# Reordering an SSM-plus-local-attention kernel: part A's corrections and outputs interleaved anew, the sine table and some loads moved, negated maxima spread by ScalarE

## The chip, the cores and the metric

The kernel runs on one core of a Trainium2 chip. The metric is the device time of one execution in microseconds (us); lower is better. An execution also has a mean granted TensorE clock, written here as a share of full speed (1.0, 0.989, ...). Times are compared at the same clock wherever that is possible, and the text says where it is not.

Engines: PE is TensorE (PEld its weight loads), DVE is VectorE, ACT is ScalarE, POOL is GpSimd, SP is SyncE, which here only issues DMAs.

## The reference

Two independent layers read their own input of 2048 positions by 448 channels; their results are concatenated.

```python
def _A_ref(x, Lambda_re, ..., Dskip):              # state space layer, P = 448 complex states
    Lam_bar = exp(exp(log_dt) * Lam)
    Bu = einsum("bld,pd->blp", x, B_bar)
    for t in range(L):                             # 2048 steps
        h = Lam_bar * h + Bu[:, t, :];  hs.append(h)
    return 2.0 * einsum("blp,dp->bld", stack(hs), Cmat).real + x * Dskip

def _B_ref(x, wqkv, wo):                           # dilated sliding attention
    q, k, v = split(x @ wqkv)                      # 16 heads of 28
    # each position sees 8 positions: itself and 2, 4, ... 14 before it
    attn = softmax(where(mask, q . k[pos - 2w] * scale, -1e9))
    return (sum over w of attn[w] * v[pos - 2w]) @ wo
```

## The kernel before

The instructions of PE, DVE, ACT and SP are issued in program order, written by hand in one function, `plan`. Each engine works through its queue in that order, so an instruction that has to wait blocks all that stand behind it on the same engine (in experiment 9 one correction waits 1.02 us at the head of PE's queue, and the matmuls behind it come late: DVE then stands 1.30 us for them). `run(gen, n)` emits the next n pieces of a generator: `fill` are query and key projections, `vp` value projections, `tb` the sine and cosine tables of part A, `sb` part A's input matrix, `pv` the products of attention and values on DVE.

Part A treats the 2048 positions as 128 chunks of 16. A position in a chunk is 4a + b. `local(b, m)` computes states within four positions for one of seven state blocks m (PE, evicted by ACT). `last`, `rot`, `scan`, `back` carry the state between chunks (PE and DVE alternately). `groups` then adds the carried state to the states b = 3 (PE, then DVE), `correct(b, ...)` to those of b = 0, 1, 2, and `y(a, b)` makes the output of one position.

```python
def max_r(self, c):                    # part B: the negated maximum over the 8 window places
    V.tensor_reduce(mx[:], ..., op=ALU.max, axis=mybir.AxisListType.X, negate=True)
    V.tensor_copy(self.mxb[:], mx[:].unsqueeze(2).to_broadcast([NCH, 4, W, H]))   # spread to 8

def correct(self, b, add, ms):
    for m in ms:
        st = add == "V"
        if not st:                                             # "A": PE adds the old state itself,
            nc.tensor.matmul(ps, lhsT=cx.ident[:], rhs=h_, start=True, stop=False)
        ...                                                    # matmul with the carried states
        if st: nc.vector.tensor_tensor(h_, ps, h_, op=ALU.add) # "V": DVE adds
        else:  nc.scalar.copy(h_, ps)                          # "A": ACT only copies

# ---- plan(), cuts marked ----
    for g, which in first:                 # first four projections of part B
        b.proj_m(0, g, which, [3])
        b.proj_e(0, g, which, "A")         # evicted by ACT
    p0 = proj(0, (2, 3))
    run(tb)                                # sine table load and three sines on ACT
    run(p0, 3)
    ...
    run(sb, 7)
    for j in range(0, T, 3):               # softmax normalisation: PE transposes, DVE divides
        b.norm(j)
        run(vp, 2)
    run(vp, 16)
    a.load_c()
    b.load_wo()
    a.setup_c()                            # DMA transposes of C
    pv = chain(b.pv(0, 4), b.pv(4, 8), b.pv(8, 12), b.pv(12, 14), b.pv(14, 16))
    for ms in ((0, 1), (2, 3)):
        loc(*((b_, m) for b_ in (0, 2, 1, 3) for m in ms))
    run(pv, 20)                            # each pv() ends with the DMA transposes into oT
    ...
    a.rot(r_[1], 0)
    a.scan(r_[1])
    a.groups(range(2, 4))
    b.out(2)
    run(pv, 1)
    a.correct(1, "A", range(0, 4))
    a.back(rb[1])
    a.correct(0, "A", range(0, 4))
    run(pv, 1)
    a.groups(range(4, 7))
    a.correct(1, "A", range(4, 7))
    a.correct(0, "A", range(4, 7))
    for a_ in range(4):
        a.y(a_, 3)
    run(pv, 8)
    a.correct(2, "V", range(7))
    ...
    for a_ in range(4):
        a.y(a_, 2)
    b.out(12)
    run(pv, 99)
    b.out(14, "AV")
```

Of the kernel before, what the change touches and what calls it, by code (L numbers as in the profile page):

```python
# [17 lines left out]
D = 448  # L18
# [74 lines left out]
class PartB:  # L93
# [5 lines left out]

    def load_x(self, c):  # L100
        if c == 0:
            self.xT = self.pool.tile([NCH, KT, S], bf16, name="xbT", tag="xT")
        sl = slice(c * CH, (c + 1) * CH)
        x_ = self.B_x[0][sl, :]
        self.nc.sync.dma_start_transpose(out=self.xT[:, 0:3, sl], in_=x_[:, 0:3 * NCH])
        self.nc.sync.dma_start_transpose(out=self.xT[:, 3, sl], in_=x_[:, D - NCH:D])

# [165 lines left out]
    def max_r(self, c):  # L273
        V, pool = self.nc.vector, self.pool
        mx = pool.tile([NCH, 4, H], bf16, name="mx", tag="mx", bufs=2)
        self.mxb = pool.tile([NCH, 4, W, H], bf16, name="mxb", tag="mxb", bufs=2)
        V.tensor_reduce(mx[:], self.pt[:].rearrange("p n (w h) -> p n h w", h=H), op=ALU.max,
                        axis=mybir.AxisListType.X, negate=True)
        V.tensor_copy(self.mxb[:], mx[:].unsqueeze(2).to_broadcast([NCH, 4, W, H]))

# [72 lines left out]

    def out(self, j, engs="AA"):
        nc, i, oT = self.nc, j % 4, self.oT[j - j % 4]
        yb = self.pool.tile([NCH, 2, D], bf16, name="yb", tag="yb", bufs=2)
        for n in range(2):
            ps = self.cx.ps([NCH, D], f32, "wo_ps", "lg")
            for k in range(KT):
                nc.tensor.matmul(ps[:], lhsT=oT[:, NSL * (i // 2) + 3 * n + k, :], rhs=self.wo_p[:, KT * n + k, :],  # L360
                                 start=(k == 0), stop=(k == KT - 1))
            self.cx.ev(engs[n], yb[:, n, :], ps[:])
        nc.sync.dma_start(self.out_b[:, j:j + 2, :], yb[:])


class PartA:
# [94 lines left out]
    def tables(self):  # L461
# [10 lines left out]
        self.rho = sm("rho")  # L472
        nc.scalar.activation(self.rho[:], at2[:, 0, :], ACT.Exp, scale=float(T))
        turn = sm("turn")
        V.tensor_scalar(turn[:], at2[:, 1, :], T / TWO_PI, None, op0=ALU.mult)
# [9 lines left out]
        nc.scalar.activation(shE[:], fr[:], ACT.Sin, scale=math.pi)  # L485
        nc.scalar.activation(sn[:], fr[:, :, NCH:], ACT.Sin, scale=-TWO_PI)
        nc.scalar.activation(self.sinE[:], fr[:, :, 0:NCH], ACT.Sin, scale=self.sgn[:])
        yield
# [14 lines left out]
    def params_g(self):  # L503
        nc, G, ident = self.nc, self.nc.vector, self.cx.ident
        lre, lim, rden, Scat, dsk = self.lre, self.lim, self.rden, self.Scat, self.dsk
        la_re, la_im = self.pw_re[:, 0, :], self.pw_im[:, 0, :]
# [13 lines left out]
        G.tensor_tensor(g_im[:], g_im[:], rden[:], op=ALU.mult)  # L520
        self.mat("g", self.rot_rows("Sg", g_re, g_im)[:], G)
        self.Dg = self.pool.tile([NCH, KT, NCH], bf16, name="Dg")
        for k in range(KT):
            nc.scalar.activation(self.Dg[:, k, :], ident[:], ACT.Copy, scale=dsk[:, k:k + 1])

# [24 lines left out]
    def setup_b(self, engs):  # L550
        nc, cx, pool = self.nc, self.cx, self.pool
        self.Bcat = pool.tile([NCH, KT, NM, NCH], bf16, name="Bcat")
        for i in range(NM):
            pt = cx.ps([NCH, KT, NCH], f32, "pt_b", "pt")
            for k in range(KT):
                nc.tensor.matmul(pt[:, k, :], lhsT=self.bX[:, i, KOFF[k]:KOFF[k] + NCH], rhs=self.mats["g"][:, i, :],
                                 start=(k == 0), stop=(k == KT - 1), skip_group_check=True)
            cx.ev(engs[i % len(engs)], self.Bcat[:, :, i, :], pt[:])
            if i == NM - 1:
                nc.gpsimd.memset(self.Bcat[0:PL, 3], 0.0)  # L560
            yield
# [127 lines left out]
def body(ctx: ExitStack, tc: tile.TileContext, A_x, A_Lre, A_Lim, A_Bre, A_Bim, A_Cre, A_Cim, A_logdt, A_Dskip,  # L689
# [7 lines left out]
    a = PartA(cx, A_x, A_Lre, A_Lim, A_Bre, A_Bim, A_Cre, A_Cim, A_logdt, A_Dskip, out_v[:, :, 0:D])  # L697
    b.load_w(1, nc.sync)
    a.load_params()
    b.load_w(0, nc.scalar)  # L700
    b.load_x(0)
    b.load_wt()
# [15 lines left out]
def run(gen, n=1):  # L718
    for _ in range(n):
        next(gen, None)  # L720


def plan(a, b, cx, pool):
# [25 lines left out]
    run(tb)  # L749
    first = [(g, which) for g in (0, 1) for which in (1, 0)]  # L750
    for g, which in first:
        b.proj_m(0, g, which, range(3))
    for g, which in first:
        b.proj_m(0, g, which, [3])
        b.proj_e(0, g, which, "A")
    p0 = proj(0, (2, 3))
    run(tb)
    run(p0, 3)
    pr = [None, None]
    for g in range(NG):  # L760
        for s in range(2):
            pr[s] = b.prod(0, s, g, g + 1)
            if g == 2 and s == 0:
                b.prod_t(0)
    run(fill, 7)
    b.sums(0, 0, pr[0])
    run(fill, 1)
    b.sums(0, 1, pr[1])
    run(tb, 2)
    run(xl, 4)  # L770
    b.vd = pool.tile([NCH, TJ, DH, H], bf16, name="vd", tag="vd")
    b.zero_halo(b.vd)
    p = b.prod(1, 0)
    b.prod_t(1)
    run(fill, 2)
    b.max_t(0)
    b.max_r(0)
    run(fill, 4)
    b.sums(1, 0, p)
    b.max_s(0)  # L780
    p = b.prod(1, 1)
    a.skip()
    a.params_g()
    run(fill, 3)
    b.sums(1, 1, p)
    p = b.prod(2, 0)
    b.prod_t(2)
    run(fill, 1)
    b.max_t(1)
    b.max_r(1)  # L790
    run(fill, 3)
    b.sums(2, 0, p)
    b.max_s(1)
    p = b.prod(2, 1)
    a.params_m([0], nc.vector)
    run(vp, 3)
    b.sums(2, 1, p)
# [7 lines left out]
    run(sb, 1)  # L805
    b.sums(3, 0, p)
    b.max_s(2)
    p = b.prod(3, 1)
    run(sb, 2)
    run(vp, 2)  # L810
    b.sums(3, 1, p)
    run(vp, 1)
    run(sb, 1)
    b.max_t(3)
    a.alloc()
    a.params_m([1, 2], nc.vector)
    b.max_r(3)
    a.params_m([3, 4], nc.vector)
    run(vp, 1)
    b.max_s(3)  # L820
    run(vp, 1)
    run(sb, 7)

    def loc(*bm):
        for b_, m in bm:
            a.local(b_, m)

    for j in range(0, T, 3):
        b.norm(j)
        run(vp, 2)  # L830
    run(vp, 16)
    a.load_c()
    b.load_wo()
    a.setup_c()
    pv = chain(b.pv(0, 4), b.pv(4, 8), b.pv(8, 12), b.pv(12, 14), b.pv(14, 16))
    for ms in ((0, 1), (2, 3)):
        loc(*((b_, m) for b_ in (0, 2, 1, 3) for m in ms))
    run(pv, 20)
    a.scan_alloc()
# [10 lines left out]
    a.back(rb[0])  # L850
    run(pv, 4)
    a.last(r[1])
    run(pv, 1)
    a.groups(range(0, 2))
    b.out(0)
    a.rot(r_[1], 0)
    a.scan(r_[1])
    a.groups(range(2, 4))
    b.out(2)
    run(pv, 1)  # L860
    a.correct(1, "A", range(0, 4))
    a.back(rb[1])
    a.correct(0, "A", range(0, 4))
    run(pv, 1)
    a.groups(range(4, 7))
    a.correct(1, "A", range(4, 7))
    a.correct(0, "A", range(4, 7))
    for a_ in range(4):
        a.y(a_, 3)
    run(pv, 8)  # L870
    a.correct(2, "V", range(7))
    for a_ in range(4):
        a.y(a_, 1)
    run(pv, 8)
    b.out(4)
    b.out(6)
    for a_ in range(4):
        a.y(a_, 0)
    run(pv, 15)
    b.out(8)  # L880
    b.out(10)
    for a_ in range(4):
        a.y(a_, 2)
    b.out(12)
    run(pv, 99)
    b.out(14, "AV")

# [30 lines left out]
```

## Time and profile before

| | before |
|---|---|
| time, median of three executions | 153.34 us (153.12 to 153.38) |
| PE busy | 137.3 us, 90% |
| DVE busy | 132.5 us, 87% |
| first product of attention and values on DVE | 65.93 us |
| last matmul ends | 147.96 us |

The first view is the page's line of busy times: engine, us, share of the span, instructions.

```profile
PE 137.3 (90%) x910; PEld 71.4 (47%) x917; DVE 132.5 (87%) x185; ACT 85.1 (56%) x167; POOL 19.4 (13%) x59
```

Two engines are nearly full, so the averages do not say which one limits. The table of windows does. Its columns are the window and its length, then the busy us (and instructions) of PE, PEld, DVE, ACT and POOL, the granted clock, the DMA share and GB/s.

```profile
20.00:40.00 20.00, 19.11 (x156) 8.43 (x158) 19.53 (x32) 15.88 (x35) 3.39 (x8) 1.00 0.32 63
40.00:66.00 26.00, 23.14 (x217) 15.49 (x217) 23.89 (x28) 16.75 (x34) 0.97 (x2) 1.00 0.32 75
66.00:92.00 26.00, 25.90 (x129) 12.12 (x130) 25.97 (x30) 14.53 (x25) 0.00 (x0) 1.00 0.54 114
```

From 20 to 66 us DVE is busy for 43.4 of 46 us and PE for 42.3. From 66 to 92 us both are full. What can be gained lies therefore in the gaps and in work that can be taken off both. The timeline shows the gaps. Its columns are start, duration (us), engine, source line, operation, output and inputs, shapes, count; the bracket is the idle time of that engine just before, and what ended it.

```profile
12.69 1.28 ACT L485 ACT_TABLE_LOAD   x1
13.98 0.98 ACT L485 ACTIVATE shE<-fr 128x931 f32<-128x931 f32 x1
16.54 1.89 PE L192 MATMUL qk_ps<-xbT,wqkv_nat 128*128 128x512 bf16 x8 [1.68 <-ACT kT L83]
17.27 1.25 DVE L238 TENSOR_TENSOR pr<-qT,kT 128x2048 bf16<-128x2048 bf16 x1 [0.71 <-ACT qT L83]
...
60.86 0.46 DVE L303 RECIPROCAL rec<-tp 128x48 f32<-128x48 f32 x1 [0.64 <-PE tp L300]
62.57 0.46 DVE L303 RECIPROCAL rec<-tp 128x48 f32<-128x48 f32 x1 [0.66 <-PE tp L300]
65.93 1.08 DVE L320 TENSOR_TENSOR pvb<-attn,vd 128x1792 bf16<-128x1792 bf16 x1
...
98.20 1.69 PE L360 MATMUL wo_ps<-wo_p,oT 128*128 128x448 bf16 x8 [1.02 <-DMA oT<-pvb]
...
146.27 1.69 PE L360 MATMUL wo_ps<-wo_p,oT 128*128 128x448 bf16 x8 [0.72 <-ACT oT L351]
148.00 0.62 DVE L88 CAST yb<-wo_ps 128x448 bf16<-128x448 f32 x1 [1.39 <-PE wo_ps L360]
```

ScalarE loads a table and makes sines in the midst of the first evictions, and PE (1.68 us) and DVE (0.71 us) wait for those evictions. DVE waits twice for PE in the normalisation, because two value projections stand between two steps. PE waits 1.02 us for a DMA transpose. The last output projection waits 0.72 us for the eviction of its transposed input.

### The profile page before, as it was taken

How to read it: one execution, taken by the hardware profiler on the slowest of the kernel's cores; microseconds unless marked ns; L12 is line 12 of the kernel's file. 1: busy time of each engine (PE TensorE's matmuls, PEld its weight loads, DVE VectorE, ACT ScalarE, POOL GpSimd, SP SyncE). 2: the span in 40 equal slices, each digit the busy share in tenths (PEclk: the TensorE clock that was granted, in tenths of full speed). 3: DMA queues.
4: the chain of work that ended last, by engine and by line, in shares of the span. 5: the costliest groups of instructions: out<-in, count | busy, mean ns of one | idle time of the engine just before them, and what ended most of it. 6: DMA issues, size and time to landing. Idle time of an engine off the chain costs nothing.

```text
span 151.8 us, 2532 instructions
## 1 busy us (share of the span) xinstructions
PE 137.3 (90%) x910; PEld 71.4 (47%) x917; DVE 132.5 (87%) x185; ACT 85.1 (56%) x167; POOL 19.4 (13%) x59
## 2 busy tenths in 40 slices
PE   6899599997999789899999999699999899999980
PEld 5243244442466557644445444354554455555530
DVE  0298799999999988799999999998899999999701
ACT  3129996799678558544564544249852126254350
POOL 8189992000000001000000000000000000000000
PEclk9999999999999999999999999999999999999999
DMA  4999991222222142529762358612511013929321
GB/s 114 252 213 196 190 193 35 36 62 44 43 60 44 39 135 55 146 43 226 109 114 67 70 130 110 121 60 73 109 35 60 30 60 102 233 91 151 128 91 60
DMA packets 42282, 15.67 MB, mean 103 GB/s; under 512 B 34770, under 2 KB 41824, under 8 KB 42269
## 3 DMA queue, kind: packets, MB, share of 16 engines
q1 hardware_dynamic: 41806, 15.16, 45.5%
q10 hardware_dynamic: 463, 0.35, 1.2%
q8 instruction: 7, 0.11, 0.3%
q14 instruction: 6, 0.05, 0.1%
HBM read 3.62 MB, written 3.67 MB: 48 GB/s over the span
## 4 chain that ended last, share of the span: by engine, by line
PE 70%; DVE 11%; ACT 11%; DMA 4%; issue 2%; SPq 0%; DVEq 0%
PE u_ps L584 16%; PE y_ps L681 14%; PE qk_ps L192 10%; PE v_ps L218 6%; PE wo_ps L360 6%; DMA xbT<-in_B_x_dram 4%; ACT kT L83 3%; PE lg L254 3%; PE y_ps L678 2%; ACT qT L83 2%; DVE pr L238 2%; PE u_ps L587 2%; PE co L656 2%; PE co L660 2%; DVE u L662 2%
## 5 line engine op out<-in xcount | busy, mean ns | idle before, releaser
L332 DVE TENSOR_TENSOR pvb<-pvb,pvt 128x1792 bf16<-128x1792 bf16 (+1 forms) x35 | 31.3, 895 | 0.1
L320 DVE TENSOR_TENSOR pvt<-attn,vd 128x1792 bf16<-128x1792 bf16 (+1 forms) x35 | 30.9, 895 | 0.0
L238 DVE TENSOR_TENSOR pr<-qT,kT 128x2048 bf16<-128x2048 bf16 (+1 forms) x12 | 27.3, 2299 | 1.1 <-ACT qT L83 0.7
L584 PE MATMUL u_ps<-xaT,Bcat 128*128 128x512 bf16 x109 | 26.5, 379 | 0.2
L192 PE MATMUL qk_ps<-xbT,wqkv_nat 128*128 128x512 bf16 x93 | 22.4, 379 | 2.9 <-ACT kT L83 2.1
L681 PE MATMUL y_ps<-C,u 128*128 128x448 bf16 x112 | 23.8, 353 | 0.0
L684 ACT CAST ya<-y_ps 128x448 bf16<-128x448 f32 x16 | 8.5, 532 | 18.5 <-PE y_ps L681 18.5
L592 ACT CAST u<-u_ps 128x512 bf16<-128x512 f32 x21 | 12.3, 585 | 10.4 <-PE u_ps L584 7.0
L584 PEld LDWEIGHTS <-Bcat 128*128 128x128 bf16 x112 | 10.8, 98 | 12.8
L192 PEld LDWEIGHTS <-wqkv_nat 128*128 128x128 bf16 x96 | 8.9, 97 | 13.8 <-issue 4.3
L360 PE MATMUL wo_ps<-wo_p,oT 128*128 128x448 bf16 x64 | 13.2, 352 | 1.7 <-DMA oT<-pvb 1.0
L218 PE MATMUL v_ps<-wqkv_nat,xbT 128*128 128x448 bf16 x64 | 13.9, 355 | 0.0
L681 PEld LDWEIGHTS <-u 128*128 128x128 bf16 x112 | 9.8, 98 | 7.3
L83 ACT CAST kT<-qk_ps 128x512 bf16<-128x512 f32 (+3 forms) x23 | 10.5, 458 | 4.1 <-PE qk_ps L192 3.9
L83 ACT CAST yb<-wo_ps 128x448 bf16<-128x448 f32 x15 | 8.0, 532 | 7.9 <-PE wo_ps L360 7.9
L83 ACT CAST qT<-qk_ps 128x512 bf16<-128x512 f32 (+1 forms) x20 | 9.9, 502 | 2.1 <-PE qk_ps L192 2.0
L83 ACT CAST vd<-v_ps 128x448 bf16<-128x448 f32 x16 | 8.5, 535 | 3.1 <-PE v_ps L218 3.1
L218 PEld LDWEIGHTS <-xbT 128*128 128x128 bf16 x64 | 8.5, 146 | 2.4 <-issue 0.4
L360 PEld LDWEIGHTS <-oT 128*128 128x128 bf16 x64 | 6.0, 97 | 7.5 <-DMA oT<-pvb 1.2
L664 ACT CAST u<-co 128x512 bf16<-128x512 f32 x14 | 7.3, 613 | 0.8 <-PE co L660 0.7
L254 PE MATMUL lg<-pr,ones 128*32 128x512 bf16 x96 | 6.7, 382 | 0.9 <-DVE pr L238 0.9
L590 ACT CAST u<-u_ps 128x512 bf16<-128x512 f32 x7 | 4.1, 585 | 5.0 <-PE u_ps L589 4.3
(164 smaller groups left out, 176.8 us busy)
## 6 DMA issues: line engine op xcount, KB each, us to landing
out_dram<-yb SPq DMA_DIRECT2D x8, 224.0 KB, 2.3
out_dram<-ya SPq DMA_DIRECT2D x16, 112.0 KB, 1.7
vd<-vd SPq DMA_DIRECT2D x2, 392.0 KB, 4.0
wqkv_nat<-in_B_wqkv_dram SPq DMA_DIRECT2D x2, 336.0 KB
wo_p<-in_B_wo_dram SPq DMA_DIRECT2D x16, 42.0 KB, 1.9
vd<-vd SPq DMA_DIRECT2D x1, 588.0 KB
xaT<-in_A_x_dram SPq DMA_TRANSPOSE x32, 2.6
bX<-in_A_B_re_dram SPq DMA_DIRECT2D x1, 392.0 KB, 4.5
```

Source lines behind the costliest of these rows:

```text
L83: nc.scalar.copy(out, in_)
L192: self.nc.tensor.matmul(self.ps_t[g, which][:], lhsT=wv[:, k], rhs=self.xT[:, k, c * CH:(c + 1) * CH], start=(k == 0), stop=(k == KT - 1))
L218: nc.tensor.matmul(ps[:], lhsT=xv[:, k, j, :], rhs=self.wn[:, k, 2, :], start=(k == 0), stop=(k == KT - 1))
L238: self.nc.vector.tensor_tensor(pr[:, :, g0:g1, :], self.qT[:, c, g0:g1].unsqueeze(1).to_broadcast([NCH, 4, n, CH]), self.windows(self.kT[: ...
L254: nc.tensor.matmul(lg[NW * t:NW * (t + 1), :], lhsT=self.ones[:, g, win], rhs=pr[:, 3 - t, g, :], start=(s == 0 and g == 0), stop=False, s ...
L320: V.tensor_tensor(buf(w) if w else acc, self.at[:, w, j0:j1, :].unsqueeze(2).to_broadcast([NCH, n, DH, H]), self.vd[:, off:off + n], op=AL ...
L332: V.tensor_tensor(acc, acc, buf(w), op=ALU.add)
L360: nc.tensor.matmul(ps[:], lhsT=oT[:, NSL * (i // 2) + 3 * n + k, :], rhs=self.wo_p[:, KT * n + k, :], start=(k == 0), stop=(k == KT - 1))
L584: nc.tensor.matmul(ps4[:], lhsT=self.Bcat[:, k, m, :], rhs=self.xT[:, b, k], start=(k == 0), stop=(b % 2 == 0 and k == KT - 1))
L592: nc.scalar.copy(self.h[b][:, m, :], ps)
L681: nc.tensor.matmul(ps[:], lhsT=self.state(m, a, b), rhs=self.C[:, m, :], start=False, stop=(m == NM - 1), skip_group_check=True)
L684: nc.scalar.copy(ya[:], ps[:])
```

## The change

The change makes no new algorithm. It moves work so that these gaps are filled, moves four small copies from DVE to ACT, and splits the last eviction. The core of the diff, with cuts marked:

```diff
-        V.tensor_copy(self.mxb[:], mx[:].unsqueeze(2).to_broadcast([NCH, 4, W, H]))
+        self.nc.scalar.copy(self.mxb[:], mx[:].unsqueeze(2).to_broadcast([NCH, 4, W, H]))
 ... tables():
         nc.scalar.activation(self.rho[:], at2[:, 0, :], ACT.Exp, scale=float(T))
+        nc.scalar.activation(self.tload[:], self.tload[:], ACT.Sin)    # table load, early
 ... a yield between the sines, so that they can be spread ...
 ... body():
-    b.load_w(1, nc.sync)
+    b.load_w(1, nc.scalar)
     a.load_params()
-    b.load_w(0, nc.scalar)
-    b.load_x(0)
+    b.load_x(0, (0,))
+    b.load_w(0, nc.sync)
+    b.load_x(0, (1,))
 ... plan():
-    run(tb)
-    run(p0, 3)
+    run(proj(0, (2, 3)), 3)
 ...
-    run(fill, 7)
+    run(fill, 2)
+    run(tb)
+    run(fill, 5)
 ...
+    loc((0, 0))
+    b.max_s(3)
+    run(vp, 1)
+    loc((0, 1))
     for j in range(0, T, 3):
         b.norm(j)
-        run(vp, 2)
+        run(vp, 1)
 ...
-    a.setup_c()
 ...
-    run(pv, 20)
+    a.skip_mats()
+    run(pv, 18)
+    a.setup_c()
 ... around the second scan, groups, corrections and pv alternate one by one:
     a.scan(r_[1])
-    a.groups(range(2, 4))
     b.out(2)
+    a.correct(1, "A", (0,))
+    a.groups((3,))
+    a.correct(1, "A", (1, 2))
+    a.back(rb[1])
 ...
-    a.correct(2, "V", range(7))
+    for i, (a_, b_) in enumerate(((0, 1), (1, 1), ..., (3, 0))):
+        a.y(a_, b_)
+        if i < NM:
+            a.correct(2, "AV"[i % 2], (i,))      # four of seven no longer on DVE
 ...
-    b.out(14, "AV")
+    a.y(3, 2)                                    # one part A output in front of the last projection
+    b.out(14, True)                              # each last eviction halved between ACT and DVE
```

More of the change, by code (lines that the diff above doesn't have):

```diff
@@ L98, in __init__, with load_x @@
         self.lg, self.oT, self.ps_t = {}, {}, {}
-    def load_x(self, c):
-        if c == 0:
+    def load_x(self, c, parts=(0, 1)):
+        if c == 0 and 0 in parts:
             self.xT = self.pool.tile([NCH, KT, S], bf16, name="xbT", tag="xT")
@@ L104, in load_x @@
         x_ = self.B_x[0][sl, :]
-        self.nc.sync.dma_start_transpose(out=self.xT[:, 0:3, sl], in_=x_[:, 0:3 * NCH])
-        self.nc.sync.dma_start_transpose(out=self.xT[:, 3, sl], in_=x_[:, D - NCH:D])
+        if 0 in parts:
+            self.nc.sync.dma_start_transpose(out=self.xT[:, 0:3, sl], in_=x_[:, 0:3 * NCH])
+        if 1 in parts:
+            self.nc.sync.dma_start_transpose(out=self.xT[:, 3, sl], in_=x_[:, D - NCH:D])
     def load_w(self, which, q):
@@ L352, in turn_p, with out @@
         nc.vector.tensor_copy(oT[:, 4:NSL], pt[:, 4:NSL])
-    def out(self, j, engs="AA"):
+    def out(self, j, split=False):
         nc, i, oT = self.nc, j % 4, self.oT[j - j % 4]
@@ L361, in out @@
                                  start=(k == 0), stop=(k == KT - 1))
-            self.cx.ev(engs[n], yb[:, n, :], ps[:])
-        nc.sync.dma_start(self.out_b[:, j:j + 2, :], yb[:])
+            if split:
+                nc.scalar.copy(yb[:, n, 0:D // 2], ps[:, 0:D // 2])
+                nc.vector.tensor_copy(yb[:, n, D // 2:], ps[:, D // 2:])
+                nc.sync.dma_start(self.out_b[:, j + n, :], yb[:, n, :])
+            else:
+                nc.scalar.copy(yb[:, n, :], ps[:])
+        if not split:
+            nc.sync.dma_start(self.out_b[:, j:j + 2, :], yb[:])
 class PartA:
@@ L486, in tables @@
         nc.scalar.activation(sn[:], fr[:, :, NCH:], ACT.Sin, scale=-TWO_PI)
+        yield
         nc.scalar.activation(self.sinE[:], fr[:, :, 0:NCH], ACT.Sin, scale=self.sgn[:])
@@ L503, in params_g @@
     def params_g(self):
-        nc, G, ident = self.nc, self.nc.vector, self.cx.ident
-        lre, lim, rden, Scat, dsk = self.lre, self.lim, self.rden, self.Scat, self.dsk
+        G = self.nc.vector
+        lre, lim, rden = self.lre, self.lim, self.rden
         la_re, la_im = self.pw_re[:, 0, :], self.pw_im[:, 0, :]
@@ L521, in params_g, with skip_mats @@
         self.mat("g", self.rot_rows("Sg", g_re, g_im)[:], G)
+    def skip_mats(self):
         self.Dg = self.pool.tile([NCH, KT, NCH], bf16, name="Dg")
         for k in range(KT):
-            nc.scalar.activation(self.Dg[:, k, :], ident[:], ACT.Copy, scale=dsk[:, k:k + 1])
+            self.nc.scalar.activation(self.Dg[:, k, :], self.cx.ident[:], ACT.Copy, scale=self.dsk[:, k:k + 1])
     def params_m(self, ks, eng):
@@ L558, in setup_b @@
             cx.ev(engs[i % len(engs)], self.Bcat[:, :, i, :], pt[:])
-            if i == NM - 1:
-                nc.gpsimd.memset(self.Bcat[0:PL, 3], 0.0)
+            nc.gpsimd.memset(self.Bcat[0:PL, 3, i, :], 0.0)
             yield
@@ L749, in plan @@
     run(tb)
-    first = [(g, which) for g in (0, 1) for which in (1, 0)]
+    first = [(g, which) for which in (1, 0) for g in (0, 1)]
     for g, which in first:
         b.proj_m(0, g, which, range(3))
-    for g, which in first:
+    for g, which in (first[0], first[2], first[1], first[3]):
         b.proj_m(0, g, which, [3])
         b.proj_e(0, g, which, "A")
-    p0 = proj(0, (2, 3))
-    run(tb)
-    run(p0, 3)
+    run(proj(0, (2, 3)), 3)
     pr = [None, None]
@@ L768, in plan @@
     b.sums(0, 1, pr[1])
-    run(tb, 2)
+    p = b.prod(1, 0)
+    b.prod_t(1)
     run(xl, 4)
@@ L772, in plan @@
     b.zero_halo(b.vd)
-    p = b.prod(1, 0)
-    b.prod_t(1)
     run(fill, 2)
+    run(tb)
     b.max_t(0)
+    run(tb)
     b.max_r(0)
@@ L781, in plan @@
     p = b.prod(1, 1)
-    a.skip()
-    a.params_g()
     run(fill, 3)
@@ L786, in plan @@
     p = b.prod(2, 0)
+    a.skip()
+    a.params_g()
     b.prod_t(2)
-    run(fill, 1)
+    run(fill, 2)
     b.max_t(1)
     b.max_r(1)
-    run(fill, 3)
+    run(fill, 2)
     b.sums(2, 0, p)
+    run(vp, 2)
     b.max_s(1)
     p = b.prod(2, 1)
-    a.params_m([0], nc.vector)
-    run(vp, 3)
+    run(vp, 1)
     b.sums(2, 1, p)
@@ L806, in plan @@
     b.sums(3, 0, p)
+    run(vp, 1)
     b.max_s(2)
     p = b.prod(3, 1)
-    run(sb, 2)
+    run(sb, 1)
     run(vp, 2)
+    run(sb, 1)
     b.sums(3, 1, p)
@@ L815, in plan @@
     a.alloc()
-    a.params_m([1, 2], nc.vector)
+    a.params_m([0], nc.vector)
     b.max_r(3)
-    a.params_m([3, 4], nc.vector)
-    run(vp, 1)
-    b.max_s(3)
-    run(vp, 1)
-    run(sb, 7)
+    a.params_m([1, 2, 3, 4], nc.vector)
     def loc(*bm):
@@ L826, in loc @@
             a.local(b_, m)
+    run(vp, 1)
+    run(sb, 7)
+    loc((0, 0))
+    b.max_s(3)
+    run(vp, 1)
+    loc((0, 1))
     for j in range(0, T, 3):
         b.norm(j)
-        run(vp, 2)
+        run(vp, 1)
     run(vp, 16)
@@ L833, in plan @@
     b.load_wo()
+    pv = chain(b.pv(0, 4), b.pv(4, 8), b.pv(8, 12), b.pv(12, 14), b.pv(14, 16))
+    loc((2, 0), (2, 1), (1, 0), (1, 1), (0, 2), (0, 3), (3, 0), (3, 1))
+    loc(*((b_, m) for b_ in (2, 1, 3) for m in (2, 3)))
+    a.skip_mats()
+    run(pv, 18)
     a.setup_c()
-    pv = chain(b.pv(0, 4), b.pv(4, 8), b.pv(8, 12), b.pv(12, 14), b.pv(14, 16))
-    for ms in ((0, 1), (2, 3)):
-        loc(*((b_, m) for b_ in (0, 2, 1, 3) for m in ms))
-    run(pv, 20)
     a.scan_alloc()
@@ L850, in plan @@
     a.back(rb[0])
-    run(pv, 4)
+    run(pv, 3)
     a.last(r[1])
+    run(pv, 2)
+    a.groups((0,))
+    b.out(0)
+    a.groups((1,))
     run(pv, 1)
-    a.groups(range(0, 2))
-    b.out(0)
     a.rot(r_[1], 0)
+    a.groups((2,))
     a.scan(r_[1])
-    a.groups(range(2, 4))
     b.out(2)
+    a.correct(1, "A", (0,))
+    a.groups((3,))
+    a.correct(1, "A", (1, 2))
+    a.back(rb[1])
     run(pv, 1)
-    a.correct(1, "A", range(0, 4))
-    a.back(rb[1])
-    a.correct(0, "A", range(0, 4))
+    a.groups((4,))
     run(pv, 1)
-    a.groups(range(4, 7))
-    a.correct(1, "A", range(4, 7))
-    a.correct(0, "A", range(4, 7))
+    a.correct(1, "A", (3,))
+    a.correct(0, "A", (0,))
+    a.groups((5,))
+    run(pv, 1)
+    a.correct(0, "A", (1,))
+    a.correct(1, "A", (4,))
+    a.groups((6,))
+    run(pv, 1)
+    a.correct(0, "A", (2,))
+    a.correct(1, "A", (5, 6))
     for a_ in range(4):
         a.y(a_, 3)
-    run(pv, 8)
-    a.correct(2, "V", range(7))
-    for a_ in range(4):
-        a.y(a_, 1)
-    run(pv, 8)
-    b.out(4)
-    b.out(6)
-    for a_ in range(4):
-        a.y(a_, 0)
-    run(pv, 15)
+        a.correct(0, "A", (3 + a_,))
+    run(pv, 12)
+    for i, (a_, b_) in enumerate(((0, 1), (1, 1), (2, 1), (3, 1), (0, 0), (1, 0), (2, 0), (3, 0))):
+        a.y(a_, b_)
+        if i < NM:
+            a.correct(2, "AV"[i % 2], (i,))
+            run(pv, 1 + i // 4)
+        if i in (3, 6):
+            run(pv, 2)
+            b.out(4 + 2 * (i // 6))
+    run(pv, 60 - 18 - 4 - 3 - 2 - 5 - 12 - 14)
+    a.y(0, 2)
+    a.y(1, 2)
     b.out(8)
     b.out(10)
-    for a_ in range(4):
-        a.y(a_, 2)
+    a.y(2, 2)
     b.out(12)
     run(pv, 99)
-    b.out(14, "AV")
+    a.y(3, 2)
+    b.out(14, True)
 kernel = body
```

## The prediction

> **What bounds the kernel.** Two engines in turn. The busy table gives PE 137.3 us (90%), DVE 132.5 us (87%), ACT 85.1 us (56%) of a 151.8 us span. By stage (busy time per stretch): from 20 to 66 us DVE is busy 43.4 of 46 us and PE has gaps behind it (waits of 0.89 us for pr, 0.54 us for mxb); from 66 to 92 us both are full; after 104 us PE runs on with few gaps to 147.96 us. What counts is when DVE reaches its products of attention and v (first one at 65.93 us) (rotations and scans queue behind), then how much PE work and how many PE gaps follow.
>
> **Costs, from the timeline and the groups.**
> 1. Sine: at 12.69 us ScalarE loads the sine table (1.28 us) and makes sine tables (about 2 us) amid evictions; PE then stands 1.67 and 0.46 us, DVE 0.71 and 0.23 us. The change loads the table while ScalarE idles (8.4 to 10.6 us) and spreads the sines. [...] PE gains over 2 us there, but DVE only about 1.0.
> 2. First loads: the first projection waits until 7.61 us for the transposed x. Moving it first should win 0 to 0.5 us for PE. But the parameter loads now queue behind a weight load, so DVE's parameter chain (to 11.4 us) may slip 0.4 us. [...] they are at 99% from 7.6 to 20 us, so I count zero.
> 3. Maxima: four copies of 0.29 us leave DVE (0.9 to 1.1 us of critical DVE time); ScalarE takes about 0.6 us each (estimate from its 0.59 us copy of 128x512).
> 4. Normalisation: one v projection between steps instead of two removes DVE waits of 0.64 and 0.66 us. But DVE should idle about 1.5 us (0.5 before) ahead of the last maximum. Net for 1 to 4: products start near 63.7 us, 2.3 us earlier.
> 5. Two local blocks (1.7 us of PE) run earlier in DVE-bound time. The output transposes go ahead of those of C, so PE's 1.02 us wait for oT goes. PE will wait 1 to 3 us near the second scan, which DVE ends at about 100 us (102.8 before).
> 6. State-2 corrections: four of seven go from DVE (0.6 us each) to PE (0.22 us more each, +0.9 us) and ScalarE; three PE gaps of 0.22 us go.
> 7. End: a projection of 1.5 us fills the 0.72 us gap at 145.5 us; halved evictions (0.62 to about 0.35 us) and a smaller last store shorten the tail by about 0.6 us.
>
> **Sum.** PE's last matmul ends near 144.2 instead of 147.96 us; with the tail, span about 147.2, time 148.6 us (3.1% faster). Range 146.3 to 150.8. Chances: faster by over 2% 0.78, within 2% 0.20, slower 0.02.
>
> **What would show it.** First product of attention and v near 63.7 us. No PE gap over 0.5 us between 8 and 20 us. PE busy up by about 0.9 us, DVE busy down by about 3.5. No PE wait for oT near 97 us. Remaining PE waits around 97 to 102 us, released by DVE. DVE's last product ending near 137 us, well ahead of PE.
>
> **What would make it wrong.** ScalarE standing in its queue for DVE's maxima, holding back evictions and so PE; corrections waiting for group additions longer than I count; PE held by the state-2 corrections left on DVE; or, the other way, fewer hidden PE gaps than I carry over.

Two passages are cut from points 1 and 2. Neither was a term of the sum, which came to 144.2 us for the end of PE's last matmul, 147.2 us of span and 148.6 us of time: point 1 rests on the table load's 1.28 us in the profile of before, and point 2 counts zero. "They" in point 2 are the core's 16 DMA engines, which that profile shows at a share of 0.99 from 7.6 to 20 us. The 0.22 us of point 6 is the distance of the starts of two such matmuls there (102.22 and 102.43 us).

## The result, and the profile after

| | before | changed |
|---|---|---|
| time, median | 153.36 us (four executions) | 149.31 us (148.04 to 153.69, four executions) |
| ratio of fast runs | 1 | 0.9663, 95% interval 0.9639 to 0.9686 |
| executions and their clock | 153.12 to 153.40, 1.0 in the profile | 148.04 and 148.24 at 1.0; 150.38 at 0.989; 153.69 at 0.978 |

A ratio is the mean time of one kernel's fast runs over that of the other's of the same rounds, so it is not quite the ratio of the medians quoted. The kernel is 3.4% faster by that ratio. But the four executions of the changed kernel are not alike. The one that was profiled is that at 0.989. A later series of the same kernel had four executions of 147.95 to 148.48 us, all at clock 1.0 and one of them profiled, and ratio 0.9673 (0.9654 to 0.9691). I call this later profile the clean one. At full clock the changed kernel takes 148.2 us, the mean of six executions.

The first fence is from the first profile of the changed kernel, at 0.989: busy times and clock by fortieths of the span from the page, then the window around the second scan. The line numbers are those of the changed kernel.

```profile
PE 138.6 (93%) x921; PEld 72.3 (49%) x921; DVE 129.1 (87%) x178; ACT 88.4 (59%) x177; POOL 23.8 (16%) x65
PEclk9999999999999999999999999996899999999999
92.00:106.00 14.00, 11.97 (x67) 6.08 (x65) 12.95 (x21) 6.58 (x13) 0.00 (x0) 0.88 0.36 90
```

DVE has 3.4 us less to do than before. In the clock row a 6 and an 8 stand for a stretch from 101.7 to 105.1 us in which the clock was at half (each digit is the mean of a slice of 3.7 us). The timeline of the same profile shows the lines that answer to those shown of before.

```profile
9.51 1.28 ACT L482 ACT_TABLE_LOAD   x1
...
53.80 0.69 DVE L279 TENSOR_REDUCE mx<-pt_m 128x64 bf16<-128x512 bf16 x1 [1.49 <-PE pt_m L273]
...
63.70 1.08 DVE L322 TENSOR_TENSOR pvb<-attn,vd 128x1792 bf16<-128x1792 bf16 x1
...
98.45 0.38 PE L667 MATMUL co<-u,ident 128*128 128x512 bf16 x1 [0.36 <-DVE u L658]
99.99 0.32 PE L633 MATMUL bakB<-rt,ident 128*128 128x384 bf16 x1 [0.95 <-DVE rt L643]
101.35 0.51 PE L656 MATMUL gt<-u,mat 128*128 128x384 bf16 x3 [0.57 <-ACT u L649]
102.09 0.63 PE L671 MATMUL co<-u,mat 128*128 128x512 bf16 x1
...
143.45 1.68 PE L362 MATMUL wo_ps<-wo_p,oT 128*128 128x448 bf16 x8
```

The table load takes 1.28 us as before, and now ends (at 10.79 us) before the first eviction starts (11.04 us). Products of attention and values begin at 63.70 instead of 65.93 us. The last output projection (at 143.45 us) has no wait in front of it. New are three waits of PE close together, 0.36, 0.95 and 0.57 us, around the second scan, and after them a matmul of 512 columns takes 0.63 us. In the clean profile the same waits are there, but the same matmul takes 0.38 us:

```profile
99.40 0.32 PE L633 MATMUL bakB<-rt,ident 128*128 128x384 bf16 x1 [0.95 <-DVE rt L643]
102.50 0.38 PE L671 MATMUL co<-u,mat 128*128 128x512 bf16 x1
125.71 0.69 DVE L673 TENSOR_TENSOR u<-co,u 128x512 bf16<-128x512 f32 x1 [1.76 <-PE co L669]
143.62 0.39 DVE L366 CAST yb<-wo_ps 128x224 bf16<-128x224 f32 x1 [0.32 <-ACT yb L365]
```

The clean profile's PE ends at 143.21 us and its span is 146.8 us, against 147.96 and 151.8 us before. Its third line is a wait that the prediction did not count: DVE stands 1.76 us for a correction of PE.

### The profile page after: what moved, and what is told of

Its sections match the earlier page's. It is cut to its first block, busy times and chain, and to the rows that moved or that the text cites. A ratio compares the mean times of both kernels' runs of the same rounds, so it can differ in the third digit from the quotient of the medians.

```text
span 148.7 us, 2556 instructions
## 1 busy us (share of the span) xinstructions
PE 138.6 (93%) x921; PEld 72.3 (49%) x921; DVE 129.1 (87%) x178; ACT 88.4 (59%) x177; POOL 23.8 (16%) x65
## 4 chain that ended last, share of the span: by engine, by line
PE 41%; DVE 32%; SPq 9%; DMA 7%; issue 4%; ACT 3%; ACTq 1%; DVEq 0%
PE y_ps L692 14%; PE qk_ps L194 9%; DVE pr L240 7%; DVE pvt L322 7%; PE wo_ps L362 6%; DVE pvb L334 5%; DMA vd<-vd 4%; SPq L415 3%; SPq L416 3%; DMA prow<-in_A_Lambda_im_dram 3%; PE co L667 3%; DVE prt L246 2%; PE y_ps L689 2%; PE co L671 2%; PE lg L256 2%
## 5 line engine op out<-in xcount | busy, mean ns | idle before, releaser
L603 ACT CAST u<-u_ps 128x512 bf16<-128x512 f32 x21 | 12.4, 589 | 8.2 <-PE u_ps L595 4.7
L220 PE MATMUL v_ps<-wqkv_nat,xbT 128*128 128x448 bf16 x64 | 14.5, 357 | 0.0
L675 ACT CAST u<-co 128x512 bf16<-128x512 f32 x18 | 10.4, 588 | 3.3 <-PE co L671 3.2
L369 ACT CAST yb<-wo_ps 128x448 bf16<-128x448 f32 x14 | 7.5, 532 | 5.4 <-PE wo_ps L362 5.3
L178 POOL TENSOR_SCALAR_AFFINE_SELECT IS<-IS 128x16 bf16<-128x16 bf16 x8 | 9.0, 1123 | 0.4
L667 PE MATMUL co<-u,ident 128*128 128x512 bf16 x18 | 7.7, 426 | 0.4 <-DVE u L658 0.4
```

Source lines behind the costliest of these rows:

```text
L220: nc.tensor.matmul(ps[:], lhsT=xv[:, k, j, :], rhs=self.wn[:, k, 2, :], start=(k == 0), stop=(k == KT - 1))
L603: nc.scalar.copy(self.h[b][:, m, :], ps)
```

## The experiments

Each experiment takes the changed kernel and undoes or alters one part. The yardstick is the changed kernel at full clock, 148.2 us, or where a variant had no execution at full clock, its one execution at 0.989, 150.38 us; the latter is weaker, being a single one. It is also a high one: in the seven kernels that ran at both clocks, the lower clock took 1.1 to 2.2 us more, and the changed kernel's own 2.2 us is the largest of these. A cost read against 150.38 us may therefore be up to 1.1 us too small.

The changed kernel at full clock was timed on chip 14 in its later series (the first result names no chip); experiments 5, 6, 7, 9 and 11 ran on chip 13. The kernel before, which ran beside each series, had medians of 153.21 to 153.41 us, so the chips differ little.

The expectations call the runs by short labels: after_ref is the changed kernel run again (experiment 10), fill_scan and fill2 are the two fillings (9 and 10), ones_first is experiment 11; the others are loads_old, params_first, mxb_dve, locals_late, sine_old, c_first, tail_old and co2_dve for experiments 1 to 8 in order.

Start times of the first instructions vary from profile to profile by up to about 1 us (DVE's first product starts at 12.45 us in the first profile of the changed kernel and at 11.37 us in experiment 5, with the same order of loads; in the profiles with that order the parameters' transpose on PE waits 0.2 to 1.1 us for its DMA). So for the front part I use a length that this does not touch: from DVE's first product of queries and keys to its first product of attention and values.

| profile | first q·k product, us | first attention·v product, us | between |
|---|---|---|---|
| before | 11.79 | 65.93 | 54.14 |
| changed, clean | 12.04 | 63.42 | 51.38 |
| sines as before | 11.37 | 64.76 | 53.39 |
| maxima spread by DVE | 11.57 | 64.21 | 52.64 |
| first loads as before | 11.58 | 62.95 | 51.37 |
| local blocks late | 11.81 | 63.18 | 51.37 |

### 1. First loads in the old order

```diff
-    b.load_w(1, nc.scalar)
+    b.load_w(1, nc.sync)
     a.load_params()
-    b.load_x(0, (0,))
-    b.load_w(0, nc.sync)
-    b.load_x(0, (1,))
+    b.load_w(0, nc.scalar)
+    b.load_x(0)
```

> Changed kernel with the first loads in the old order (parameters first on ScalarE's queue, a weight first on SP's). Theory P: the change's load order costs time, because the parameters land 1.2 us later (7.06 against 5.87 us) and VectorE's first product starts at 12.45 instead of 11.79 us; with the old order the product starts near 11.8 us and the whole is 0.6 us faster than the changed kernel (147.5 us against 148.1). Rival X: moving x first is a gain; then undoing it makes the first projection later and the whole 0.3 to 0.6 us slower (148.5 us or more).

Measured: ratio 0.9676 (0.9636 to 0.9715). At full clock 147.78, 147.81 and 148.19 us, mean 147.9; at 0.988 two of 149.3; one slow of 153.84. With the old order the kernel is thus about 0.3 us faster than with the new one, if anything. Moving the loads won nothing.

### 2. Parameters ahead of the weight on ScalarE's queue

```diff
-    b.load_w(1, nc.scalar)
     a.load_params()
+    b.load_w(1, nc.scalar)
```

> Changed kernel, x still first on SP's queue, but the three parameter loads ahead of the weight on ScalarE's queue. Theory P: parameters land near 5.9 us again, first product of VectorE near 11.8 us, whole 0.5 to 0.8 us faster than the changed kernel (147.5 us). Rival X: the weight then lands later and the first projection with it, so no gain (148.1 us) or a loss.

Measured: four executions at full clock of 148.42 to 148.74 us, 0.4 us slower than the changed kernel; two at 0.988 and 0.989 of 150.06 and 150.13; ratio 0.9718. PE's first projection then waits 1.63 us for the weight instead, at 6.21 us, and DVE's first product starts at 12.03 us, no earlier than in the clean profile. Putting the parameters first only moves the wait to the weight.

### 3. Maxima spread by DVE again

```diff
-        self.nc.scalar.copy(self.mxb[:], mx[:].unsqueeze(2).to_broadcast([NCH, 4, W, H]))
+        V.tensor_copy(self.mxb[:], mx[:].unsqueeze(2).to_broadcast([NCH, 4, W, H]))
```

> Changed kernel with the four spreads of the maxima back on VectorE. Theory D (VectorE's progress up to its second scan near 100 us sets the time): VectorE does 4 x 0.29 us more, 3 of them without a wait behind, the first product of attention and v at 64.6 to 64.9 instead of 63.7 us, the whole 0.9 to 1.1 us slower (149.1 us). Rival E (TensorE's work and gaps set it, VectorE has slack): 148.1 us, no change, or faster, since ScalarE no longer stands waiting for maxima (6.3 us of waits).

Measured: ratio 0.984 (0.981 to 0.9871), but all five fast executions (150.42 to 151.63 us, mean 150.9) were at 0.989, so that ratio includes the loss of clock; a sixth, slow one took 154.32 us. Against the changed kernel's single execution at that clock the copies cost 0.5 us, and with the uncertainty of that yardstick 0.5 to 1.6 us; the 0.9 to 1.1 us expected lie within. The front stretch of the table grows by 1.26 us, and PE waits again for DVE:

```profile
42.85 0.83 PE L256 MATMUL lg<-pr,ones 128*32 128x512 bf16 x12 [1.14 <-DVE pr L240]
```

ScalarE's standing for the maxima, which the prediction feared, is real: the changed kernel's waits list 6.3 us in four waits.

```profile
ACT mxb L281 <- DVE mx L279: 6.3, 4, 2.6
```

(The columns are us in total, times, longest.) These waits cost nothing that can be seen: with the copies on DVE the front part is longer, not shorter.

### 4. The two local blocks late again

```diff
-    loc((0, 0))
     b.max_s(3)
     run(vp, 1)
-    loc((0, 1))
 ...
-    loc((2, 0), (2, 1), (1, 0), ...
+    loc((0, 0), (0, 1), (2, 0), (2, 1), (1, 0), ...
```

> Changed kernel with the two local blocks of state 0 put back behind the normalisation. Prediction's step 5: TensorE comes 1.7 us later to everything after, whole about 1.7 us slower (149.8 us). Rival D: TensorE waits 1.9 us for VectorE around the second scan (98 to 101 us) anyway, so the delay eats these waits and the whole is at most 0.3 us slower (148.1 to 148.4 us), the waits near 98 to 101 us shrinking to under 0.5 us.

Measured: 149.36 to 149.50 us in three executions at full clock, 1.2 us slower; two at 0.989 of 151.24 and 151.54; one slow of 154.2. The front stretch stays at 51.37 us, so the loss is behind it: PE gets to the second scan's input later, and DVE, which was never idle there before, stands for it.

```profile
93.81 0.56 DVE L627 TENSOR_TENSOR rt<-g3B,cosE 128x384 bf16<-128x384 f32 x1 [1.59 <-PE g3B L624]
```

The 1.7 us of PE work that moved were thus worth about 1.2 us: PE had room for them before 64 us, and none after.

### 5. Sine table and sines amid the first evictions again

```diff
-        nc.scalar.activation(self.tload[:], self.tload[:], ACT.Sin)
 ...
         b.proj_e(0, g, which, "A")
+    run(tb, 2)
     run(proj(0, (2, 3)), 3)
 ...  the two later run(tb) taken out
```

> Changed kernel, with the sine table loaded and all three sine activations made amid the first evictions, as before. Theory D (products on VectorE set the pace early, TensorE has slack there): VectorE's waits for ScalarE of 0.7 and 0.2 us come back, so 0.7 to 1.0 us slower than the changed kernel in runs at full clock (149.0 us). Rival E (TensorE's stop of over 2 us counts in full): 2 us or more slower (150.2 us). Rival N: early slack hides all of it, 148.1 us.

Measured: 149.79 us at full clock (one execution), 1.6 us slower; three at 0.989 of 151.55 to 151.76, 1.3 us above the single 150.38. The old PE waits are back to the hundredth, and DVE's grow:

```profile
15.96 1.89 PE L194 MATMUL qk_ps<-xbT,wqkv_nat 128*128 128x512 bf16 x8 [1.68 <-ACT kT L83]
21.72 3.36 DVE L240 TENSOR_TENSOR pr<-qT,kT 128x6144 bf16<-128x6144 bf16 x1 [1.19 <-ACT qT L83]
```

The front stretch is 2.0 us longer. The prediction gave DVE 1.0 us here, from DVE's two waits of 0.71 and 0.23 us in the profile before. In this variant DVE waits 0.57 and 0.23 us, and a further 1.19 us at 20.5 us, for the evictions that ScalarE had put off: the delay of the queue outlasts the sines. The kernel before has no such third wait, so 2.0 us is what the old sines cost in the changed kernel; what their move took off the kernel before is nearer to its two waits, 0.94 us.

### 6. Transposes of C ahead of those of the attention output

```diff
     b.load_wo()
+    a.setup_c()
 ...
     run(pv, 18)
-    a.setup_c()
```

> Changed kernel, with the four transposes of C queued before the first output transpose, as before. Theory: the output transpose is then issued near 92 instead of 86.5 us and lands near 96 us, TensorE waits 3 to 4 us for oT at the first output projection (92.7 us), VectorE's second scan slips with it, whole 2 to 4 us slower (150.1 to 152 us at full clock). Rival: the wait is hidden in TensorE's later waits for the second scan (1.9 us), less than 1 us slower.

Measured: ratio 0.9904 (0.9861 to 0.9946). No execution was at full clock; those at 0.987 to 0.989 took 151.34, 151.37 and 152.34 us, 1 to 2 us above the changed kernel's 150.38 (up to 3.1 us with the uncertainty of that yardstick); one slow took 153.68 us. PE waits for the DMA:

```profile
95.02 2.48 PE L362 MATMUL wo_ps<-wo_p,oT 128*128 128x448 bf16 x8 [2.82 <-DMA oT<-pvb]
```

With the rest of the change in place this wait is 2.82 us, against 1.02 us in the kernel before: PE comes to this product 5.0 us earlier (at 92.20 instead of 97.18 us), the DMA, which SP issues behind the four transposes of C, only 3.2 us earlier (at 91.00 instead of 94.19 us). DVE's wait of 2.80 us for PE follows from it. Here the change that shortened PE's chain raised what the order of SP's queue costs.

### 7. The old tail

```diff
+    a.y(3, 2)
     b.out(12)
     run(pv, 99)
-    a.y(3, 2)
-    b.out(14, True)
+    b.out(14)
```

> Changed kernel, with the last state projection ahead of output 12 and the last output evicted whole, as before. Theory: the gap of about 0.7 us before the last output comes back and the tail is 0.6 us longer, 1.2 to 1.4 us slower (149.4 us at full clock). Rival: since VectorE now ends 3 us before TensorE, no gap comes back and only the eviction counts, 0.3 to 0.6 us slower (148.6 us).

Measured: 149.41 and 149.70 us at 0.996, 151.38 and 150.73 us at 0.988. The tail is worth about 1.3 us at full clock, and the gap of before is back:

```profile
142.34 1.69 PE L362 MATMUL wo_ps<-wo_p,oT 128*128 128x448 bf16 x8 [0.72 <-ACT oT L353]
```

### 8. All seven state-2 corrections on DVE

```diff
-            a.correct(2, "AV"[i % 2], (i,))
+            a.correct(2, "V", (i,))
```

> Changed kernel with all seven corrections of state 2 added by VectorE (none by TensorE and ScalarE). Theory S (VectorE has slack by then: it waits 1.8 us for a correction and ends 3 us ahead of TensorE): four matmuls of 0.22 us less on TensorE, 0.5 to 0.9 us faster (147.4 us at full clock); giving four to ScalarE was then a loss. Rival L: VectorE comes to these corrections late, TensorE waits for banks, 0.5 us or more slower (148.7 us).

Measured: one execution at full clock, 147.92 us; three at 0.988 of 148.86 to 149.19; two slow of 152.98 and 153.45. DVE's wait of 1.76 us for a correction is gone, and PE waits only once for a correction of DVE, 0.2 us. The direction is that the split between PE and DVE won nothing and perhaps lost 0.3 us, but one execution at full clock does not settle it; the three at 0.988 are even 1.4 us below the single 150.38, a yardstick that is too high by up to 1.1 us.

### 9. The loss of clock, first filling

In the clock records of the changed kernel's first profile the low stretch is one single record of 3413 ns at half clock, from 101.68 to 105.09 us, right behind the waits around the second scan; the records on either side of it are at full clock. One such record in a span of 148.7 us makes a mean of 0.989, and 24 executions of experiments 1 to 8 lie at 0.987 to 0.989. In the profile of experiment 8, at 0.988, matmuls of 512 columns take 0.63 instead of 0.38 us from 100.8 to 102.7 us, behind the same wait of 0.57 us. Theory, an assumption: PE's waits around the second scan (1.9 us in the first profile) bring the half clock about in some executions. Rival: the clock falls at that time whatever PE does. To tell them apart, four more corrections were put into the waits.

```diff
     a.groups((3,))
-    a.correct(1, "A", (1, 2))
+    a.correct(1, "A", (1,))
+    a.correct(0, "A", (0, 1))
+    a.correct(1, "A", (2,))
+    a.correct(0, "A", (2,))
     a.back(rb[1])
     run(pv, 1)
+    a.correct(1, "A", (3,))
     a.groups((4,))
 ...  taken out where they stood later
```

> Changed kernel, with four corrections moved up into TensorE's waits around the second scan (98 to 101.3 us). Theory: the waits of 0.95 and 0.57 us are filled, 1.0 to 1.4 us faster (146.9 us at full clock); and since the half-clock window of 3.4 us that some runs show just after these waits (clock 0.989 over the run, near 101 us) follows a stretch in which TensorE was mostly idle, no run shows a window there any more. Rival: the window falls there whatever TensorE does (a fixed time after start), so runs at clock 0.989 stay as common (about half), and are 1.5 to 2.3 us slower.

Measured: 149.11 to 150.02 us, ratio 0.976 (0.9737 to 0.9783). None of six executions had the lower clock, but the kernel was 1.4 us slower than the changed one at full clock. A correction was placed too early, in front of what it needed and of what others needed:

```profile
99.76 0.38 PE L667 MATMUL co<-u,ident 128*128 128x512 bf16 x1 [1.02 <-DVE u L658]
105.54 0.38 PE L671 MATMUL co<-u,mat 128*128 128x512 bf16 x1 [0.88 <-DVE u L658]
```

A matmul that waits for DVE at the head of PE's queue blocks the matmuls of the next group addition, which DVE in turn waits for (1.30 us at 100.7 us). The waits had been moved apart, not filled.

### 10. The filling done in the right order, and the changed kernel once more

```diff
     a.groups((3,))
-    a.correct(1, "A", (1, 2))
+    a.correct(1, "A", (1,))
+    a.correct(0, "A", (0,))
+    a.correct(1, "A", (2,))
+    a.correct(0, "A", (1,))
     a.back(rb[1])
     run(pv, 1)
+    a.correct(0, "A", (2,))
     a.groups((4,))
     run(pv, 1)
     a.correct(1, "A", (3,))
-    a.correct(0, "A", (0,))
     a.groups((5,))
     run(pv, 1)
-    a.correct(0, "A", (1,))
+    a.correct(0, "A", (3,))
     a.correct(1, "A", (4,))
 ...  and so on: each correction one group addition later than the one it needs
```

> The changed kernel itself again, as a reference on the same chip and in the hope of a profile at full clock. Expected: runs at clock 1.0 near 148.1 us, others at clock 0.989 near 150 us with one half-clock window of 3.4 us near 101 us.

> Second try at filling the waits around the second scan: two corrections of state 0 before the back rotation, one after it, and every correction that needs a group's addition separated from that group by another piece of work (the first try put correction 3 of state 1 ahead of group 4 and so made VectorE wait 1.3 us and TensorE 2.8 us in all). Theory: TensorE's waits between 98 and 105 us fall from 1.9 to under 1 us, 0.5 to 1.0 us faster than the changed kernel at full clock (147.3 us), and no half-clock window near 101 us. Rival: what ends this stretch is the chain of rotation, scan, rotation and group additions itself, not TensorE's work, and then nothing is gained at full clock (148.1 us) although the windows go.

Measured, both on the same chip: the changed kernel 147.95 to 148.48 us in four executions; the filled one 146.50, 146.81, 146.91 and 147.56 us, and one slow of 152.09 us, which was the one profiled. Ratio of fast runs 0.9587 (0.9563 to 0.9611), against 0.9673 (0.9654 to 0.9691): the filled kernel beats the changed one and experiment 9. PE has no wait above 0.25 us between 95 and 106 us in its profile.

On the clock, all executions can be counted together. Of the kernels that have the waits near 100 us (the changed one and experiments 1 to 8; in experiment 6, with three of its four at that clock, the DMA wait stands in their place), 25 of 50 executions were at 0.987 to 0.989 (two of these 25 were slow ones of over 154 us). Of the three filled ones (experiments 9, 10 and 11), none of 16 was. In the two series that hold both sorts it was 11 of 22 against none of 11. Within one kernel the fast executions at that clock, and the changed kernel's 150.38 us, were 1.1 to 2.2 us longer than those at full clock. The kernel before, which runs beside the experiments, was at 0.989 in one of 42 executions (156.44 us). So the loss went with the waits, and the rival, a fixed time, does not fit these counts.

The traces add how long PE stood. Here are the 3.41 us before the half-clock record of the first profile, and two stretches of that length over the same waits in the clean one; the idle time is the length less the first busy time, PE's (the ends of matmuls are modelled):

```profile
98.26:101.67 3.41, 1.56 (x7) 0.62 (x7) 3.38 (x8) 1.58 (x3) 0.00 (x0) 1.00 0.19 67
96.76:100.17 3.41, 2.27 (x11) 0.84 (x10) 3.38 (x8) 2.14 (x4) 0.00 (x0) 1.00 0.19 67
100.17:103.59 3.42, 2.79 (x18) 1.63 (x18) 3.34 (x6) 2.24 (x5) 0.00 (x0) 1.00 0.00 0
```

In the first profile PE was idle for 1.85 of the 3.41 us, and half clock followed. The clean profile has the same waits (1.14 and 0.62 us idle in its two stretches) and kept full clock, as 20 of the 50 executions did (0.996 to 1.0); what decides between the two is not shown. The profile of experiment 6, at 0.989, has a DMA wait of 2.82 us instead, and in experiment 10's slow execution half clock comes with a wait of 2.87 us (next experiment). In experiment 9 PE's waits add up to more than in the changed kernel (2.9 against 1.9 us), but they lie further apart (1.02 us before 99.76 us, 0.88 us before 105.54 us), and none of its six executions had the lower clock. Nor does a single wait always cost the clock: the kernel before has one of 1.68 us that ends at 16.54 us, kept full clock behind it in its profile, and was at 0.989 in one of 42. How much standing costs the clock, and when, these runs do not tell.

### 11. The remaining slow executions

The profile of experiment 10's slow execution shows where its 5 us went. First the page's clock row, then PE's and GpSimd's timelines:

```profile
PEclk9999995599999999999999999999999999999998
17.58 5.86 POOL L161 TENSOR_SCALAR_AFFINE_SELECT ones<-ones 128x16 bf16<-128x16 bf16 x5
23.21 0.62 PE L256 MATMUL lg<-pr,ones 128*32 128x512 bf16 x4 [2.87 <-POOL ones L161]
28.49 1.23 DVE L246 TENSOR_TENSOR prt<-qT,kT 128x2048 bf16<-128x2048 bf16 x1 [5.39 <-issue]
```

PE waits 2.87 us for `ones`, a constant that GpSimd builds from ten small selects. The clock is then at half (the two digits of 5 in the clock row, 22.6 to 30.1 us), and DVE stands 5.39 us. The profile names no releaser; the likely one is PE, whose late sums still read the buffer of DVE's next product (the last of them ends at 28.38 us). The same selects in the profile of before and in the clean profile of the changed kernel:

```profile
14.31 2.74 POOL L159 TENSOR_SCALAR_AFFINE_SELECT ones<-ones 128x16 bf16<-128x16 bf16 x5
```

```profile
13.41 4.72 POOL L161 TENSOR_SCALAR_AFFINE_SELECT ones<-ones 128x16 bf16<-128x16 bf16 x5
```

The five selects take 2.74 us before, 4.72 us after and 5.86 us in the slow run. Before, DVE had pauses in this stretch (0.71 and 0.23 us), where the sines held up the evictions; the changed kernel closed them. Most of the single selects in the profile of before and in the changed kernel's first one show what DVE's work beside them does: in the profile of before three of them in DVE's pause at 16.6 us take 0.19 us each, and one beside a product of 128x2048 takes 1.18 us; in the changed kernel two beside such products take 1.18 us each, and one beside the product of 128x6144 3.20 us. By what means the one slows the other is not shown. In the slow run these selects also started 4.2 us later (17.58 against 13.41 us): 1.9 us because the five selects before them began at 11.00 instead of 9.14 us, and 2.3 us because those five, now beside DVE's products, took 5.34 instead of 3.03 us. So `ones` was ready at 17.85 us before, at 20.9 us in the clean profile, where PE waited 0.31 us for a part of it, and at 24.2 us in the slow run. The last experiment therefore takes the filled kernel of experiment 10 and moves `ones` ahead in GpSimd's queue.

```diff
     b.load_w(2, nc.sync)
+    b.consts()              # only ones
     a.consts()
     b.alloc()
     b.tail_w()
-    b.consts()
+    b.consts_rest()
```

> The kernel fill2 with the ones constants built earlier on GpSimd, ahead of its other start-up work. Theory G (the slow executions of 152 to 154 us come from GpSimd's selects for ones being slowed by VectorE, which pauses less than it did before): the last ones constant, ready at 24.2 us in the slow profile of fill2, at 20.9 us in the clean profile of the changed kernel and at 17.8 us before, is ready by 16 to 18 us; TensorE has no wait for GpSimd near 20 us (2.87 us in the slow profile of fill2, 0.31 us in the changed kernel); no execution is above 148.5 us; the fast ones are as fill2 or up to 0.3 us faster, 146.5 to 146.8 us. Rival: the slow executions have another cause; ones is ready early and still one execution in five or six takes 152 us or more.

Measured: 146.36 to 146.77 us in five executions, all at clock 0.997 or above; ratio 0.9553 (0.9529 to 0.9577). This is the fastest version: 4.5% faster than before, and 1.7 us below the changed kernel at full clock. Against experiment 10's fast executions (0.9563 to 0.9611) the intervals overlap, so a gain of its own is not shown. The selects now run largely before DVE's long products start (11.55 us):

```profile
8.45 2.07 POOL L161 TENSOR_SCALAR_AFFINE_SELECT ones<-ones 128x16 bf16<-128x16 bf16 x5
```

`ones` is complete at 11.0 us, earlier than the 16 to 18 us expected, and PE has no wait for GpSimd. That the earlier `ones` removes the wait is shown. That it removes the slow executions is not: in the kernels with `ones` in its old place 8 of 61 executions were slow ones of 152 us or more (six at 0.973 to 0.978, two at 0.989), so five without one would come about by chance in about half of such series. Only one slow execution was profiled, so whether the others had this cause stays open as well.

## Why the prediction was right or wrong

The time was right: 148.6 us predicted, 149.31 us the median, 148.2 us at full clock. The median fell so near partly by luck, as it mixes executions with and without the loss of clock, which the prediction did not know of. At full clock it was the sum that was right; its terms were so to different degrees. Undoing each part, at the same clock as far as there were executions, costs:

| part | predicted | measured by undoing it |
|---|---|---|
| sines (1) | 1.0 us for DVE, over 2 us for PE | 1.6 us of time, 2.0 us in DVE's front stretch |
| first loads (2) | 0 | -0.3 us (the old order is better) |
| maxima (3) | 0.9 to 1.1 us for DVE | 0.5 to 1.6 us of time (one execution to compare), 1.26 us in the front stretch |
| two local blocks (5) | 1.7 us of PE work earlier | 1.2 us |
| transposes of the attention output first (5) | 1.0 us | 1 to 3 us (one execution to compare) |
| state-2 corrections (6) | PE 0.9 us more, DVE freed | about -0.3 us (one execution) |
| end (7) | 0.72 us gap and 0.6 us of tail | 1.3 us |

Taken with their signs, and the lower ends for the maxima and the transposes, the column adds up to 5.0 us, near the 5.1 us between 153.3 and 148.2 us. That says little: two terms are lower ends, the parts were undone singly, experiments 5 and 6 show that a part can grow with the others, and the normalisation (4) and the new order around the second scan were never undone.

Point by point:

- **Start of the products.** Predicted near 63.7 us; 63.70 in the first profile, 63.42 in the clean one. The front stretch shrank by 2.76 us, predicted 2.3. DVE's waits in the profiles of before and after, and experiment 3, say from what: the 0.94 us behind the sines are gone (about 1.0 predicted), so are 1.30 us in the normalisation; the maxima's copies gave 1.26 us (0.9 to 1.1 predicted); and the wait before the last maximum grew from 0.49 to 1.49 us, as predicted. Together that is 2.5 us.
- **Gaps.** No PE gap over 0.5 us between 8 and 20 us and none for the attention output near 97 us, as said. Waits of 1 to 3 us were predicted near 97 to 102 us; they were 1.88 us in the first profile.
- **Busy times.** DVE 3.4 us less, predicted 3.5. PE rose by 1.3 us in the first profile, predicted 0.9; that one has matmuls at half clock in it, and the clean profile, which has 11 matmul records fewer, shows 136.1 us, below the 137.3 us before. So this is no test of it.
- **First loads.** Counting zero was close. The 16 DMA engines were at 0.99 from 7.6 to 20 us before and after, and changing the order of the first loads in two ways moved the time by -0.3 and +0.4 us, in experiment 2 with the wait moving to another load. The possible gain of 0 to 0.5 us did not appear. That full engines are why the order does not matter was the author's assumption.
- **End.** PE's last matmul was predicted to end at 144.2 us; it ends at 143.21 us in the clean profile. The predicted 147.2 us of span is 146.8 us there.
- **DVE's last product.** Predicted near 137 us; it ends at 138.96 us in the clean profile, still ahead of PE. DVE's wait of 1.76 us for a correction is nearly of that size; that it is the cause is not shown. The prediction looked at PE held by corrections on DVE, not at DVE held by them.
- **The step that failed: the waits near the second scan were taken for their own length only.** The prediction said "PE will wait 1 to 3 us near the second scan" and did not consider that the clock could be lost there as well. Half of the executions of such kernels (25 of 50) ran at a mean clock of 0.987 to 0.989, as one record of 3413 ns at half clock gives it, and the first profile has that record right behind the waits; the fast ones among these executions took 1.1 to 2.2 us longer. With the waits filled it was 0 of 16. For the same reason the prediction expected one time, where there are three groups of them: 148, 150 and over 152 us. The last group was not foreseen either: one execution of the four, 153.69 us, lies outside the predicted range.
- **ScalarE held by the maxima**, a named risk, happened (6.3 us) and did no harm. **Hidden gaps** fewer than carried over was the other risk; the clean time is 0.4 us below the prediction, so they were about as counted.

## What to carry to other kernels

When two engines are nearly full, cost a reordering by the gaps that it closes on each, and ask of every wait that is left whether it lies close to others, and look at the clock behind it. Here several short waits of the tensor engine (1.85 us of standing in 3.41 us) had half clock behind them in the first profile, and filling them took the slower clock from 25 of 50 executions to none of 16. Independent small matmuls were the filling, placed after what they need and never in front of what another engine waits for. A table load or other long job in an evicting engine's queue can cost more than the waits right behind it: in experiment 5 the front stretch grew by 2.0 us, where DVE's two waits right behind the sines were 0.57 and 0.23 us. And closing one engine's pauses can slow a slow helper that lived on them (here five selects on GpSimd took 4.72 instead of 2.74 us): build its constants before the busy stretch, and look at slow executions in the profile rather than only leaving them out.
